# New figures for TensorE products and per-row scaling in a kernel that schedules itself

## The chip, the cores and the metric

One Trainium2 chip, one core of it, one launch. The metric is the time of the device in microseconds (us), median of several runs.

## The reference

```python
# attention: 2 batches x 8 heads x 768 positions x 64; 4 sink keys, window 128
scores = scale * np.matmul(q, k.transpose(0, 1, 3, 2))
scores = np.where(is_sink | in_window, scores, -1e9)
a = np.exp(scores - np.max(scores, axis=-1, keepdims=True))
a = a / (np.sum(a, axis=-1, keepdims=True) + 1e-09)
x = (a @ v).transpose(0, 2, 1, 3).reshape(1536, 512)
# mixture of 4 experts, w1 512x1024, w2 1024x512, all experts for all tokens
p = domain_probs / (domain_probs.sum(-1, keepdims=True) + 1e-09)
for e in range(4):
    out += p[:, e:e + 1] * (np.maximum(x @ w1[e], 0.0) @ w2[e])
# gated layer, d_ff 1536
return (out @ w_a) * (out @ w_b) @ w_out
```

The weights of the gated layer come as 64-bit floats, passed as pairs of 32-bit integers, and are turned into 32-bit floats on the chip.

## The kernel before

**The arithmetic.** Every operand of a product is split in two rounded parts, high and low (`split`, L467), and a product is three matmuls: high by high, high by low, low by high (`three`, L956). In the trace those are `xh,uh`, `xl,uh`, `xh,ul` or `dh,hh`, `dh,hl`, `dl,hh`. The products with w1, w_a and w_b go through `seven` (L1031), which makes a 2x2 block product from seven products, with 384 columns each. The products with w2 and w_out have 512 columns (`down_tile`, L973; `Gated.tile`, L1138). Attention is done with 256 to 288 columns (`scores`, L595); for batch 0 its score products take their 64 rows of contraction straight from one head (tiles `kk`, `qh`, `ql`), and the softmax rows are multiplied by the reciprocal of their sum, a number per row (tiles `pp`, `st`; L680 ff.). The 128x128 transposes are products with `ident`.

**The stages.** There are three, each recorded and then put in order by itself. Stage 1: attention of batch 0 and the first two chunks of the experts (TensorE instructions 1 to 672 of 4845, to about 119 us). Stage 2: attention of batch 1 beside 13 items of experts on batch 0 (to about 375 us). Stage 3: the last item of batch 0, 16 items of experts on batch 1, then 24 items of the gated layer. One item (`Expert` L1085, `Gated` L1105) is a block of 256 columns of w1, or of 128 of w_a and the same 128 of w_b, with the 768 tokens of a batch.

**The weights.** For each item `ups` (L912) loads a block of w1 (`rawu<-in_w`) or of the converted w_a and w_b (`rawu<-gu`), makes four sums on POOL or DVE (`sums`), and splits them on ACT, DVE and POOL (`uh`, `ul`). The buffer `rawu` is there once, so a load can start when the item before has read it. Split weights are stored for the second batch (`ug`, `dg` for the gated layer) and loaded back. `gate_weights` (L1251) converts the 64-bit weights in stage 3, part by part: load to `raw`, six operations on `tu` (mostly DVE, some on ACT and POOL), store to `gu` or `gd`. The first gated items read `gu` as it becomes ready.

**The order.** Nothing is issued where it is written. `Plan` (L95) records each call with its operands; `note` (L177) makes a node of it, finds what it depends on, and asks `cost` (L149) for its length in ns on each engine that may do it (`either`, L118: copies on ACT or DVE, sums on POOL or DVE, scaling on ACT, DVE or POOL). Codes are T for TensorE, V for DVE, S for ACT, G for POOL and D for a DMA. `run` (L244) then gives each node a due time, worked back from TensorE's nodes, whose own times are the sum of their costs; it steps through a model of the five engines, always placing the node that can start first, the most urgent among those ready, within 8 nodes of TensorE's written order. `fits` (L279) decides there between engines. The result is one fixed order for each engine's queue; every instruction of the kernel is issued from L355 in that order. Fixed figures of the model that stay as they are: the lag between engines (`LAG`, 60 to 256 ns, and `EXTRA` 40), 2200 ns from a DMA to its user (`WAY`), and the DMA issue itself, 60 ns + 1.42 per element of a row.

So the figures of `cost` say nothing to the chip. They decide in which order, on which engine, and how far ahead of TensorE the other work stands.

Of the kernel before, what the change touches and what calls it, by code (L numbers as in the profile page):

```python
# [18 lines left out]
P = 128  # L19
# [75 lines left out]
class Plan:  # L95
# [52 lines left out]
    @staticmethod  # L148
    def cost(engine, name, args, kw):  # L149

        size = 1
        for d in kw.get("out", args[0] if args else None).shape[1:]:
            size *= d
        psum = any("PSUM" in str(getattr(v, "space", "")) for v in (*args[1:], *(v for k, v in kw.items() if k != "out")))
        if engine == "T":
            return 3 + size / 2.4 * (2 if name == "transpose" else 1)
        if engine == "V":
            fast = name in ("tensor_copy", "tensor_scalar") and not psum
            return 65 + size * (0.52 if fast else 1.04) + (55 if fast and hasattr(kw.get("scalar1"), "ap") else 0)
        if engine == "S":  # L160
            return (50 if psum else 95) + size / 1.2 + (180 if "accum_out" in kw else 0)
        return {"G": 150 + size * 2.1, "D": 60 + size * 1.42}[engine]

    @staticmethod
# [79 lines left out]
    def run(self, ahead=8):  # L244
# [46 lines left out]
        for _ in nodes:  # L291
# [42 lines left out]
            for f in x["ways"]:  # L334
                ready[f].remove(x)
            x["e"], (cost, x["calls"], shared) = e, x["ways"][e]
            x["cost"] = cost
            free[e] = now + cost
# [1282 lines left out]
```

## Time and profile before

| | |
|---|---|
| median of 3 runs | 952.56 us (951.90 to 953.61) |
| the profiled execution, its own time | 951.72 us |
| its span | 949.6 us |
| TensorE (PE) busy | 920.8 us, 97% of the span, 4845 matmuls |
| DVE, ACT, POOL busy | 741.1 (78%), 404.3 (43%), 324.2 (34%) us |
| chain that ended last | PE 77%, DVE 13%, DMA 5%, ACT 2% |

The span is what the trace covers; the profiled execution took 2.1 us more than it, and 0.84 us less than the median. A record's length is not its share of an engine: matmuls overlap, so that a 512-column matmul has a record of 0.39 us while the next starts 0.23 us after it. What a product takes is therefore read from the distance of starts in the timeline.

### The profile page before, as it was taken

How to read it: one execution, taken by the hardware profiler on the slowest of the kernel's cores; microseconds unless marked ns; L12 is line 12 of the kernel's file. 1: busy time of each engine (PE TensorE's matmuls, PEld its weight loads, DVE VectorE, ACT ScalarE, POOL GpSimd, SP SyncE). 2: the span in 40 equal slices, each digit the busy share in tenths (PEclk: the TensorE clock that was granted, in tenths of full speed). 3: DMA queues.
4: the chain of work that ended last, by engine and by line, in shares of the span. 5: the costliest groups of instructions: out<-in, count | busy, mean ns of one | idle time of the engine just before them, and what ended most of it. 6: DMA issues, size and time to landing. Idle time of an engine off the chain costs nothing.

```text
span 949.6 us, 13937 instructions
## 1 busy us (share of the span) xinstructions
PE 920.8 (97%) x4845; PEld 824.8 (87%) x4845; DVE 741.1 (78%) x1516; ACT 404.3 (43%) x946; POOL 324.2 (34%) x328
## 2 busy tenths in 40 slices
PE   7999989999999999999999999999999999999996
PEld 6778878898888888888989989999887789999995
DVE  6798789999999998997876878799898985333343
ACT  6677557766656573521222312143453453211111
POOL 3565445646544651520200110044254543110100
PEclk9699999999999999999999999999999999999998
DMA  4250068886566744587867777877778878755552
GB/s 150 93 204 25 2 211 319 289 289 233 181 232 239 287 170 154 202 314 253 304 225 284 248 263 245 289 252 250 272 257 296 285 287 314 268 199 199 201 198 93
DMA packets 84752, 215.47 MB, mean 227 GB/s; under 512 B 7872, under 2 KB 42176, under 8 KB 84672
## 3 DMA queue, kind: packets, MB, share of 16 engines
q1 hardware_dynamic: 84672, 214.49, 64.6%
q8 instruction: 40, 0.66, 0.3%
q14 instruction: 40, 0.33, 0.1%
HBM read 131.10 MB, written 83.36 MB: 226 GB/s over the span
## 4 chain that ended last, share of the span: by engine, by line
PE 77%; DVE 13%; DMA 5%; ACT 2%; issue 2%; POOL 1%; SPq 1%; DVEq 0%; ACTq 0%; POOLq 0%
PE bank L355 77%; DVE tu L355 2%; DMA rawu<-gu 2%; DVE ul L355 2%; DVE y L355 1%; DVE kk L355 1%; DVE c L355 1%; DVE pp L355 1%; DVE sums L355 1%; DVE hl L355 1%; DMA rawu<-in_w 1%; DVE st L355 1%; DMA scr<-in_dp 1%; DMA araw<-in_a 1%; SPq L355 1%
## 5 line engine op out<-in xcount | busy, mean ns | idle before, releaser
L355 PE MATMUL bank<-dh,hh 128*128 128x512 f32 x528 | 210.2, 398 | 0.0
L355 PE MATMUL bank<-dl,hh 128*128 128x512 f32 x528 | 208.5, 395 | 0.0
L355 PE MATMUL bank<-dh,hl 128*128 128x512 f32 x528 | 208.0, 394 | 0.0
L355 PE MATMUL bank<-xh,uh 128*128 128x384 f32 (+1 forms) x384 | 129.7, 338 | 0.7 <-DVE r L355 0.7
L355 PE MATMUL bank<-xl,uh 128*128 128x384 f32 (+1 forms) x384 | 127.2, 331 | 0.0
L355 PE MATMUL bank<-xh,ul 128*128 128x384 f32 (+1 forms) x384 | 127.1, 331 | 0.0
L355 PEld LDWEIGHTS bank<-dl,hh 128*128 128x128 f32 x528 | 99.0, 187 | 21.7
L355 PE MATMUL bank<-th,uh 128*128 128x384 f32 x324 | 109.7, 339 | 3.9 <-DVE c L355 2.5
L355 PEld LDWEIGHTS bank<-dh,hh 128*128 128x128 f32 x528 | 99.2, 188 | 13.9 <-issue 0.3
L355 PEld LDWEIGHTS bank<-dh,hl 128*128 128x128 f32 x528 | 99.2, 188 | 12.6
L355 PE MATMUL bank<-tl,uh 128*128 128x384 f32 x324 | 109.2, 337 | 0.1
L355 PE MATMUL bank<-th,ul 128*128 128x384 f32 x324 | 108.8, 336 | 0.0
L355 ACT ACTIVATE r<-bank 128x384 f32<-128x384 f32 x73 | 35.8, 491 | 146.5 <-PE bank L355 145.9
L355 ACT ACTIVATE hh<-c 128x384 fp32r<-128x384 f32 x98 | 50.8, 519 | 96.7 <-DVE c L355 95.5
L355 DVE TENSOR_TENSOR c<-bank,r 128x384 f32<-128x384 f32 x108 | 59.8, 554 | 35.1 <-PE bank L355 34.5
L355 DVE SCALAR_TENSOR_TENSOR y<-bank,prob,y 128x512 f32<-128x512 f32 x108 | 80.0, 744 | 7.3 <-PE bank L355 6.6
L355 DVE TENSOR_TENSOR c<-bank,u 128x384 f32<-128x384 f32 x54 | 29.9, 553 | 67.6 <-PE bank L355 64.4
L355 PEld LDWEIGHTS bank<-xh,uh 128*128 128x128 f32 x384 | 72.7, 189 | 7.3 <-issue 1.1
L355 PEld LDWEIGHTS bank<-xl,uh 128*128 128x128 f32 x384 | 72.8, 190 | 4.4
L355 PEld LDWEIGHTS bank<-xh,ul 128*128 128x128 f32 x384 | 72.7, 189 | 0.0
L355 PEld LDWEIGHTS bank<-th,uh 128*128 128x128 f32 x324 | 60.8, 188 | 9.1 <-DVE c L355 3.7
L355 POOL TENSOR_TENSOR ul<-sums,uh 128x256 fp32r<-128x256 f32 (+1 forms) x39 | 40.6, 1043 | 80.7 <-ACT uh L355 80.6
(147 smaller groups left out, 1860.5 us busy)
## 6 DMA issues: line engine op xcount, KB each, us to landing
ue<-uh SPq DMA_DIRECT2D x14, 896.0 KB, 4.3
ue<-ul SPq DMA_DIRECT2D x14, 896.0 KB, 6.1
uh<-ue SPq DMA_DIRECT2D x14, 896.0 KB, 4.8
ul<-ue SPq DMA_DIRECT2D x14, 896.0 KB, 6.8
ug<-uh SPq DMA_DIRECT2D x12, 896.0 KB, 5.4
ug<-ul SPq DMA_DIRECT2D x12, 896.0 KB, 7.8
uh<-ug SPq DMA_DIRECT2D x12, 896.0 KB, 4.7
ul<-ug SPq DMA_DIRECT2D x12, 896.0 KB, 6.8
```

The lines of the kernel that those rows point to most:

```text
L355: call(*args, **kw)
```

## The change

Only `cost` is touched. A product of N columns goes from 3 + N/2.4 to 1 + 0.4535 N, a transpose of N columns from 3 + N/1.2 to 1 + 0.84 N, a product whose weights have fewer than 128 rows gets 65 ns more, and an ACT instruction with a scale per row gets 85 ns more. In ns: 512 columns 216.3, now 233.2; 384 columns 163.0, now 175.1; 256 columns 109.7, now 117.1; a transpose of 128 columns 109.7, now 108.5; 288 columns with 64 rows 123.0, now 196.6; per-row scaling of 288 columns on ACT 335, now 420.

```diff
@@ -153,12 +153,14 @@
         if engine == "T":
-            return 3 + size / 2.4 * (2 if name == "transpose" else 1)
+            rows = kw["lhsT"].shape[0] if "lhsT" in kw else P
+            return 1 + size * (0.84 if name == "transpose" else 0.4535) + (65 if rows < P else 0)
...
         if engine == "S":
-            return (50 if psum else 95) + size / 1.2 + (180 if "accum_out" in kw else 0)
+            return (50 if psum else 95) + size / 1.2 + (180 if "accum_out" in kw else 0) + (
+                85 if hasattr(kw.get("scale"), "ap") else 0)
```

No instruction is added or taken away in the arithmetic: the matmuls are the same 4845. What moves is order, and the engine of operations that may run on two: over the program DVE has 35 instructions more and ACT 40 fewer, of which 20 and 22 lie in stage 2.

**At the start, on DVE's queue.** `scr<-scr 128x12` is the sum of the four domain probabilities, which waits for their load; `pp<-bank,pen` (an ISA row) masks a tile of scores in PSUM and frees that bank for TensorE's next score products. Before:

```order
L355 TENSOR_TENSOR kk_157<-araw_146,kk_157 128x288
L355 TENSOR_SCALAR flag<-lim 128x1
L355 TENSOR_SCALAR scr_140<-lim 128x1 x2
L355 ISA pp_151,low<-bank_99,pen 128x288
L355 ISA low 128x1
L355 ISA pp_151,low<-bank_98,pen 128x128
L355 ISA low 128x1
L355 TENSOR_REDUCE scr_140<-scr_140 128x12
L355 TENSOR_SCALAR st_152<-st_152 128x2
```

and after:

```order
L357 TENSOR_TENSOR kk_157<-araw_146,kk_157 128x288
L357 TENSOR_TENSOR vv_147<-araw_145,vv_147 128x2x2x64
L357 TENSOR_REDUCE scr_140<-scr_140 128x12
L357 TENSOR_SCALAR flag<-lim 128x1
L357 TENSOR_SCALAR st_152<-st_152 128x2
L357 ISA pp_151,low<-bank_99,pen 128x288
L357 ISA low 128x1
L357 RECIPROCAL st_152<-st_152 128x2
L357 ISA pp_151,low<-bank_98,pen 128x128
```

The sum over the probabilities now stands ahead of both maskings, where it stood behind them; a subtraction for `vv` has come to DVE as well.

**Among the first gated items, on the queue of DMA issues (SP).** `rawu<-gu_66` is the load of the converted weights of one gated item; `raw<-in_wa` and `raw<-in_wo` are loads of 64-bit weights for the conversion and `gu_70<-tu` is a store of one half of a converted block; `ug`, `dg` are stores of split weights. Before:

```order
L355 DMA dg_1_3850<-dl_180 128x512
L355 DMA dg_0_3853<-dh_171 128x512
L355 DMA rawd_158<-gd_77 128x512
L355 DMA dg_1_3854<-dl_172 128x512
L355 DMA dg_0_3857<-dh_179 128x512
L355 DMA raw_1_3827<-in_wa 128x4x256
L355 DMA gu_70<-tu_3828 512x1x128
L355 DMA rawu_163<-gu_66 128x1024
```

and after:

```order
L357 DMA raw_0_3825<-in_wo 128x1024
L357 DMA rawd_158<-gd_76 128x512
L357 DMA dg_1_3849<-dl_180 128x512
L357 DMA dg_0_3852<-dh_171 128x512
L357 DMA rawu_163<-gu_66 128x1024
L357 DMA ug_0_3850<-uh_169 128x1792
L357 DMA raw_1_3826<-in_wa 128x4x256
L357 DMA ug_1_3851<-ul_170 128x1792
L357 DMA gu_70<-tu_3827 512x1x128
```

The load of the item's weights stood behind a load and the second store of the conversion and now stands ahead of them, and the stores of `dg` and the load `rawd<-gd_77` that stood ahead of it come later. Counted in TensorE instructions written before it, this load moves from 3694 to 3638; those of blocks 65 and 67 move from 3592 to 3580 and from 3767 to 3712, and that of block 64 goes back from 3516 to 3524.

## Rows read from the trace of the kernel before

**Rows 1.** The page: span, busy time by engine, chain by engine.

```profile
span 949.6 us, 13937 instructions
...
PE 920.8 (97%) x4845; PEld 824.8 (87%) x4845; DVE 741.1 (78%) x1516; ACT 404.3 (43%) x946; POOL 324.2 (34%) x328
...
PE 77%; DVE 13%; DMA 5%; ACT 2%; issue 2%; POOL 1%; SPq 1%; DVEq 0%; ACTq 0%; POOLq 0%
```

**Rows 2.** Busy time by stretch: length, then each engine, TensorE's granted clock, DMA share, GB/s.

```profile
core 0: us, PE busy (x) PEld busy (x) DVE busy (x) ACT busy (x) POOL busy (x), PEclk, DMA share, GB/s
0.00:23.74 23.74, 17.20 (x69) 14.65 (x69) 15.31 (x77) 14.35 (x45) 9.42 (x24) 1.00 0.50 150
118.69:142.44 23.75, 20.78 (x113) 18.53 (x112) 20.27 (x38) 12.89 (x31) 10.64 (x15) 1.00 0.61 212
142.44:356.10 213.66, 211.49 (x1145) 188.41 (x1144) 203.68 (x433) 142.51 (x352) 121.19 (x123) 1.00 0.71 249
660.00:780.00 120.00, 112.70 (x582) 100.99 (x581) 108.53 (x174) 55.56 (x118) 53.88 (x46) 1.00 0.79 275
28.96:46.02 17.06, 17.06 (x66) 14.56 (x66) 10.81 (x40) 10.22 (x31) 7.42 (x8) 0.50 0.31 96
```

**Rows 3.** Timeline of PE: start, length of the record, engine, line, operation.

```profile
23.31 0.52 PE L355 MATMUL bank<-kk,qh 64*128 64x288 f32 x2
23.68 0.29 PE L355 MATMUL bank<-kk,ql 64*128 64x288 f32 x1
...
60.66 0.40 PE L355 MATMUL bank<-dh,hh 128*128 128x512 f32 x1
...
61.82 0.39 PE L355 MATMUL bank<-dl,hh 128*128 128x512 f32 x1
...
502.49 0.33 PE L355 MATMUL bank<-th,uh 128*128 128x384 f32 x1
502.66 0.33 PE L355 MATMUL bank<-tl,uh 128*128 128x384 f32 x1
```

**Rows 4.** Groups: count | busy, mean ns | idle before, and what ended it.

```profile
L355 ACT ACTIVATE pp<-pp,st 128x288 f32<-128x288 f32 (+1 forms) x79 | 33.0, 470 | 15.9 <-DVE sq L355 6.0 <-DVE st L355 6.0 <-POOL sq L355 3.6
...
L355 PE MATMUL bank<-ident,pp 128*128 128x128 f32 x176 | 29.8, 294 | 2.2 <-ACT pp L355 1.7 <-DVE pt L355 0.5
```

**Rows 5.** Waits of PE from 660 to 780 us: total, times, longest.

```profile
PE bank L355 <- ACT r L355: 3.4, 3, 2.0
PE bank L355 <- DVE c L355: 1.4, 3, 0.9
PE bank L355 <- DVE ul L355: 1.4, 1, 1.4
PE bank L355 <- ACT x L355: 1.2, 2, 0.6
```

**Rows 6.** The chain that ended last, pieces from 677 to 771 us: start, length, what.

```profile
677.26 6.62 DMA rawu<-gu
...
688.81 0.48 ACT r L355
689.34 14.97 PE bank L355 x78
...
766.48 4.39 DMA rawu<-gu
```

**Rows 7.** Timelines of DVE and PE at the start, in brackets what ended the idle time.

```profile
8.68 0.45 DVE L355 CUSTOM_DVE_ANT_0 pp<-bank,pen 128x288 f32<-128x288 f32 x1
9.05 0.08 DVE L355 DVE_READ_ACCUMULATOR2_ANT low<- 128x1 f32 x1
...
10.70 0.20 DVE L355 TENSOR_REDUCE scr<-scr 128x12 f32<-128x48 f32 x1 [1.11 <-DMA scr<-in_dp]
...
9.28 0.81 PE L355 MATMUL bank<-kk,qh 64*128 64x288 f32 x2
...
11.85 0.88 PE L355 MATMUL bank<-ident,pp 128*128 128x128 f32 x3 [0.88 <-ACT pp L355]
```

## The prediction

> **What bounds the kernel now.** I read the page first: TensorE is busy 920.8 of 949.6 us, and the chain that ended last is TensorE for 77% [rows 1]. Nothing in the change makes a product shorter, and none is dropped, so all that can be won is time in which TensorE stands, 949.6 - 920.8 = 28.8 us, and what a changed order does to its clock. The second view is the busy time by stretch, which tells where it stands [rows 2]: 23.74 - 17.20 = 6.5 us at the start, 23.75 - 20.78 = 3.0 us where stage 1 hands over to stage 2, 213.66 - 211.49 = 2.2 us over the whole of stage 2 that follows, and 120.00 - 112.70 = 7.3 us between 660 and 780 us, where the gated items begin. These are 19.0 of the 28.8 us. The third view is the timeline of TensorE, for the true distance of products: six 512-column products start from 60.66 to 61.82, which is 1.16 / 5 = 0.232 us each; the 384-column ones start 0.17 us apart; two 64-row ones take 23.68 - 23.31 = 0.37 us, 0.185 each [rows 3]. The new figures (233, 175 and 197 ns) are these; the old ones (216, 163 and 123) were too short by 7% and by a third. The figure for scaling per row goes from 335 to 420 ns, towards a record of 470 in the mean [rows 4]. So the change makes the scheduler's TensorE run at the chip's pace. Before, the model's TensorE ran ahead of the real one; the other engines were planned against a faster engine than there is. A plan with too fast a TensorE shifts everything it cannot finish in time to the most urgent order and sees engines as full that are not. With a slower TensorE it sees more room per product on the other engines, and sets work earlier as counted in products.
>
> [...]
>
> **Part by part.** All five terms are changes of TensorE's standing time, since only order moves.
>
> *Start.* DVE used to mask the 288-column scores at 8.68, ahead of the sum over the probabilities, which waited 1.11 us for its load and ran at 10.70; the bank so freed let TensorE begin score products at 9.28 [rows 7]. Now the sum stands ahead, and DVE takes its queue in order: the masking can start at about 10.70 + 0.2 and two small operations, some 11.1, ends 0.45 later, and the products start at 11.5 instead of 9.28, 2.2 us later. Of this, 0.88 us is time in which TensorE would have waited anyway, before the transposes at 11.85 [rows 7]. That leaves 2.2 - 0.88 = **+1.3 us**. Bounds: 0, if the transposes' own chain stays in time and the products fit behind them; +2.2, if the softmax on ACT slips by as much as the masking.
>
> *Later softmax of stage 1.* The transposes stood for 2.2 us in all for `pp` and `pt`, 0.88 of it the wait just named [rows 4, 7], so 1.3 us are left, at two places. With 64-row products and scaling at their true length, the order puts more TensorE work between a scaling and its transpose there (7 instructions instead of 1 at the tightest). New places with 3 appear elsewhere. I take **-0.9**, with bounds -1.3 and 0.
>
> *Handover, 119 to 142 us.* TensorE stands 3.0 us [rows 2], waiting for DVE. Of DVE's operations there, one copy of a product's result goes to ACT, and one copy and one sum come to DVE. ACT is busy for 12.89 of 23.75 us there, DVE for 20.27. I take **-1.0**, a third; bounds -2.0 (one of the 3.0 us stays with loads that no figure moves) and 0.
>
> *Stage 2, 142 to 356 us.* DVE gets 20 instructions more, ACT 22 fewer. At DVE's mean of 203.68 / 433 = 0.47 us that is 9.4 us of work for an engine with 213.66 - 203.68 = 10.0 us left by its records [rows 2]. But records overlap: the masking of 8.68 lasts by its record to 9.13, and the next instruction starts at 9.05 [rows 7], 0.37 us after it, 18% less than 0.45. If all do so, DVE is held for 167 of 214 us, and 9.4 more fit. I take **0**; bounds -2.2 (all the standing time goes) and +9.4.
>
> *First gated items, 660 to 780 us.* TensorE's waits here sum to 3.4 + 1.4 + 1.4 + 1.2 = 7.4 us, for `r` and `x` from ACT, `c` and `ul` from DVE [rows 5]. They are late because ACT and DVE stand in their queues at splits of weights whose load has just landed: the chain goes through a load of 6.62 us at 677.26, ends with ACT's copy `r` at 688.81, and TensorE goes on at 689.34 [rows 6]. In the new order the loads of blocks 65, 66 and 67 stand 12, 56 and 55 TensorE instructions earlier. One instruction is 120.00 / 582 = 0.206 us here [rows 2], so these are 2.5, 11.5 and 11.3 us, more than any wait of this group. The load of block 64 goes back by 8, or 1.6 us; the longest wait, 2.0 us, hangs on it and stays. On the queue of DMA issues the load of block 66 now passes a store of the conversion, which comes later: that block of converted weights is ready later, and what is late next is a later gated item's load. I set 0.4 us for it, next to the smallest wait of the group (0.6). So 7.4 - 2.0 - 0.4 = 5.0, **-5.0 us**. Bounds: -7.3 (all of it) and 0 (the next rival).
>
> Elsewhere TensorE hardly stands, and I set nothing. Each engine's instructions there move within the time that TensorE covers; if that cover went, the price is that of stage 2's upper bound, which the first rival has.
>
> **Sum.** 1.3 - 0.9 - 1.0 + 0 - 5.0 = -5.6 us against the profiled execution's 951.72, which is 946.1. That execution is 0.84 us under the median of the runs, so I forecast 947.0 us as the median. The likely bounds of this case are 942 to 951.
>
> **The rivals.**
>
> *DVE becomes the bound in stage 2 (slower).* Place: 142 to 356 us. The 20 instructions more take 9.4 us, and 10.0 us are free by the records. From the point at which the free pieces are shorter than one instruction each, or lie where DVE waits for TensorE, the 9.4 us go through to TensorE, which waits there for `hl` and `c`. For it: DVE at 95%. Against it: the overlap, and that TensorE stood for only 2.2 us at that load. Time: 951.72 + 1.3 - 0.9 - 1.0 + 9.4 - 5.0 = 955.5, 956.4 as a median.
>
> *Nothing comes of stage 3 (no change).* The waits of 660 to 780 us hang on loads of 4.39 to 6.62 us [rows 6], and the scheduler still reckons with the same short time for them. If a load's issue is held by its buffer, an earlier place in the queue brings nothing. Then the handover and the gated items give 0, and the sum is +1.3 - 0.9 = +0.4: 952.1, 953.0 as a median. For it: the load is the longest piece of the chain there. Against: the waits sit behind the splits, which move apart from the loads.
>
> [...]
>
> *The figures overshoot.* If products took the 216 ns of the old formula wherever no record is missing, the new plan would set work 8% late against the real TensorE, and the standing time of 660 to 780 us would double: 951.72 + 1.3 + 7.3 = 960.3, 961.1 as a median. [...] Rows 3 are against it at three sizes.
>
> **How the numbers follow.** A measurement of this kernel can tell about 0.2%, 1.9 us, from no change: faster is below 950.7, slower above 954.5. Chances: the forecast 0.55; nothing from stage 3 0.17; DVE as the bound 0.17; the clock 0.09; overshoot 0.02. Faster: 0.50 of the forecast, 0.04 of the second, 0.09 of the clock, 0.63. Same: 0.05 and 0.10, 0.15. Slower: 0.17, 0.02 and 0.03 of the second, 0.22. The range of 940 to 956.5 leaves out two thirds of the clock's case, the lowest corner of the forecast, half of DVE's case and the overshoot, about 0.18.
>
> **What would show it.** Right: in the profile of the changed kernel TensorE is busy over 117 of the 120 us of the first gated items and the waits for `r`, `c` and `x` there are under 3 us; the score products of the second head start after 11 us. DVE in stage 2 is busy longer than before by some 9 us, and TensorE no less. Wrong: TensorE's busy time between 142 and 356 us falls by several us with waits for DVE (DVE as the bound); the waits in the gated items stay near 7 us (nothing from stage 3); the stretch of clock 0.50 is gone or longer (clock); products of 512 columns start nearer than 0.23 us (overshoot).

## The result, and the profile after

| | before | with the change |
|---|---|---|
| median | 952.23 us (8 runs, 949.05 to 957.55) | 960.53 us (8 runs, 959.96 to 963.64) |
| profiled execution, span | 951.72, 949.6 us | 961.12, 959.3 us |

The ratio is 1.0085, with a 95% interval of 1.0064 to 1.0105: the change makes the kernel 0.85% slower. The forecast was 947.0 with a range of 940 to 956.5, so the result lies outside the range and on the other side.

The head of the page with the change, for [rows 1]:

```profile
span 959.3 us, 13934 instructions
...
PE 925.5 (96%) x4845; PEld 822.6 (86%) x4845; DVE 756.3 (79%) x1551; ACT 387.4 (40%) x906; POOL 325.8 (34%) x332
...
PE 42%; DVE 33%; DMA 15%; issue 3%; POOL 3%; ACT 2%; SPq 1%; DVEq 0%; POOLq 0%; ACTq 0%
```

TensorE's part of the chain that ended last fell from 77% to 42%, DVE's rose from 13% to 33% and that of DMAs from 5% to 15%. Before, TensorE led and the rest kept up; now long pieces of that chain run through DVE and through transfers. Where time was lost, the busy time by stretch tells. With the change, for [rows 2]:

```profile
0.00:23.74 23.74, 15.00 (x56) 12.49 (x57) 13.89 (x68) 13.37 (x40) 10.28 (x24) 1.00 0.49 149
118.69:142.44 23.75, 21.92 (x118) 19.58 (x117) 20.41 (x40) 14.64 (x35) 10.42 (x14) 1.00 0.68 237
142.44:356.10 213.66, 208.59 (x1119) 183.65 (x1118) 207.06 (x435) 132.14 (x322) 116.04 (x119) 1.00 0.69 245
375.00:660.00 285.00, 281.25 (x1402) 249.27 (x1400) 237.83 (x426) 68.86 (x130) 43.78 (x35) 1.00 0.72 250
660.00:780.00 120.00, 118.22 (x607) 105.78 (x608) 110.04 (x174) 52.55 (x113) 62.68 (x55) 1.00 0.81 281
```

The fourth of these stretches was not looked at ahead of the change, since TensorE did not stand in it at all; in the trace of before it is

```profile
375.00:660.00 285.00, 285.00 (x1436) 256.53 (x1436) 235.53 (x416) 79.87 (x152) 55.37 (x45) 1.00 0.75 260
```

Read the counts in brackets rather than the busy time. In 142 to 356 us TensorE did 26 products fewer than before (1119 against 1145), in 375 to 660 us 34 fewer (1402 against 1436), and in 660 to 780 us 25 more (607 against 582). At 213.66 / 1145 = 0.187 us a product the first is 4.9 us, at 285.00 / 1436 = 0.198 the second is 6.7 us, both lost; at 0.206 us the third is 5.2 us won. The busy time shows only 2.9 and 3.75 us of the losses: a 512-column product has a record of 0.39 us and the next can start after 0.23, so a stop of up to 0.16 us hides in the record of the product ahead.

Since both programs have the same 4845 matmuls in nearly the same order, the loss can be followed exactly: take the start of TensorE's instruction n (counted from 0) in either trace and subtract. Against before, the change stands at -0.1 us at instruction 672 (end of stage 1), at +5.5 at 1994 (end of stage 2), at +12.7 at 3560 (685 us in before), at +7.0 at 3960, at +8.1 at 4100, and stays there to TensorE's last instruction. The span is 9.7 us longer: the other 1.6 us are lost behind that, while the last results are stored. That tail differs from before's by -0.3 to +1.9 us in the other runs, and none of them goes after it. The experiments below are told in these four pieces: **stage 1** (to 672), **stage 2** (672 to 1994), **early stage 3** (1994 to 3560) and **gated start** (3560 to 4100).

Three stops in early stage 3 show how products are lost there. One of them, in the timeline of all engines of the changed kernel:

```profile
422.67 0.39 PE L357 MATMUL bank<-dh,hh 128*128 128x512 f32 x1
...
422.89 0.39 PE L357 MATMUL bank<-dh,hl 128*128 128x512 f32 x1
...
423.13 0.40 PE L357 MATMUL bank<-dl,hh 128*128 128x512 f32 x1
...
423.34 0.74 DVE L357 SCALAR_TENSOR_TENSOR y<-bank,prob,y 128x512 f32<-128x512 f32 x1
...
424.00 0.68 DVE L357 TENSOR_TENSOR tu<-tu 128x512 f32<-128x512 f32 x1
...
424.23 0.34 PE L357 MATMUL bank<-xh,ul 128*128 128x384 f32 x1
...
424.60 0.55 DVE L357 TENSOR_TENSOR c<-bank,r 128x384 f32<-128x384 f32 x1
...
425.21 0.45 PE L357 MATMUL bank<-th,uh 128*128 128x384 f32 x1 [0.64 <-DVE c L357]
```

TensorE needs the bank that `c<-bank,r` reads. That stands on DVE behind a `y` and behind a step of the weight conversion (`tu<-tu`), each 0.6 to 0.7 us; DVE has no idle time there, it is only late. No transfer made it late: DVE's first wait for one in this stage ends at 438.01 us, and by then 3.1 of the 7.2 us are lost. One reason can be seen at an earlier stop, at 391.74 us. DVE in the trace of before, then all engines with the change:

```profile
382.14 0.95 DVE L355 TENSOR_TENSOR xl<-x,xh 128x768 fp32r<-128x768 f32 x1
383.09 0.56 DVE L355 TENSOR_TENSOR c<-bank,r 128x384 f32<-128x384 f32 x1
```

```profile
386.98 1.85 POOL L357 TENSOR_TENSOR tl<-x,th 128x768 fp32r<-128x768 f32 x1 [3.39 <-ACT th L357]
...
387.28 2.36 DVE L357 TENSOR_TENSOR xl<-x,xh 128x768 fp32r<-128x768 f32 x1
...
389.57 1.65 DVE L357 TENSOR_TENSOR x<-x 128x384 f32<-128x384 f32 x1
...
391.14 0.55 DVE L357 TENSOR_TENSOR c<-bank,r 128x384 f32<-128x384 f32 x1
...
391.74 0.44 PE L357 MATMUL bank<-th,uh 128*128 128x384 f32 x1 [0.75 <-DVE c L357]
```

With the change `xl` starts while POOL is at `tl`, and takes 2.36 us instead of 0.95; `c` stands behind it.

The other 4.1 us are lost after 438.01 us, and there DVE does stand for transfers. A stop of that kind:

```profile
570.75 0.43 DVE L357 TENSOR_SCALAR tu<-raw 128x512 int32<-128x512 int32 x1 [2.38 <-DMA gd<-tu]
...
572.88 0.55 DVE L357 TENSOR_TENSOR c<-bank,r 128x384 f32<-128x384 f32 x1
...
573.49 0.55 PE L357 MATMUL bank<-ident,y 128*128 128x128 f32 x3 [0.93 <-DVE c L357]
```

DVE's own waits for stores from 375 to 660 us, with the change and before:

```profile
DVE tu L357 <- DMA gu<-tu: 14.1, 10, 2.6
DVE tu L357 <- DMA gd<-tu: 7.0, 5, 2.4
```

```profile
DVE tu L355 <- DMA gu<-tu: 1.7, 4, 0.5
DVE tu L355 <- DMA gd<-tu: 1.4, 2, 0.9
```

The one buffer `tu` is free for the next part when its store has landed; DVE arrives at that part too early and stands, and all that is queued behind it stands with it.

At the start, for [rows 7], timelines of DVE and PE with the change:

```profile
10.82 0.20 DVE L357 TENSOR_REDUCE scr<-scr 128x12 f32<-128x48 f32 x1 [1.74 <-DMA scr<-in_dp]
10.94 0.14 DVE L357 TENSOR_SCALAR flag<-lim 128x1 f32<-128x1 f32 x1
11.00 0.79 DVE L357 TENSOR_SCALAR st<-st 128x2 f32<-128x2 f32 x1
11.70 0.45 DVE L357 CUSTOM_DVE_ANT_0 pp<-bank,pen 128x288 f32<-128x288 f32 x1
...
12.30 0.82 PE L357 MATMUL bank<-kk,qh 64*128 64x288 f32 x2 [2.90 <-DVE st L357]
```

The masking runs at 11.70 instead of 8.68, and TensorE takes up the second head at 12.30 instead of 9.28, as forecast but 0.8 us later still.

And the gain that was forecast is there. TensorE's waits from 660 to 780 us, for [rows 5]:

```profile
PE bank L357 <- ACT x L357: 0.6, 1, 0.6
PE bank L357 <- DVE r L357: 0.6, 1, 0.6
PE bank L357 <- ACT r L357: 0.5, 1, 0.5
PE bank L357 <- DVE c L357: 0.2, 1, 0.2
```

1.9 us where 7.4 stood.

### The profile page after: what moved, and what is told of

The parts are those of the page before. It is cut to its first block, busy times and chain, and to the rows that moved or that the text cites. A ratio compares the mean times of both kernels' runs of the same rounds, so it can differ in the third digit from the quotient of the medians.

```text
span 959.3 us, 13934 instructions
## 1 busy us (share of the span) xinstructions
PE 925.5 (96%) x4845; PEld 822.6 (86%) x4845; DVE 756.3 (79%) x1551; ACT 387.4 (40%) x906; POOL 325.8 (34%) x332
## 4 chain that ended last, share of the span: by engine, by line
PE 42%; DVE 33%; DMA 15%; issue 3%; POOL 3%; ACT 2%; SPq 1%; DVEq 0%; POOLq 0%; ACTq 0%
PE bank L357 42%; DVE tu L357 9%; DMA gu<-tu 6%; DVE y L357 4%; DVE hl L357 3%; DMA rawu<-in_w 3%; DVE c L357 3%; DMA rawu<-gu 3%; DVE ul L357 2%; DMA gd<-tu 2%; DVE sums L357 2%; POOL tu L357 1%; DVE x L357 1%; DVE kk L357 1%; POOL sums L357 1%
## 5 line engine op out<-in xcount | busy, mean ns | idle before, releaser
L357 ACT ACTIVATE hh<-c 128x384 fp32r<-128x384 f32 x94 | 48.8, 519 | 135.7 <-DVE c L357 135.6
L357 POOL TENSOR_TENSOR tu<-tu 128x512 f32<-128x512 f32 x15 | 19.7, 1311 | 177.4 <-DVE tu L357 177.4
```

The lines of the kernel that those rows point to most:

```text
L357: call(*args, **kw)
```

## The experiments

Three theories stood against each other at first. **Pace**: what counts in the table is TensorE's pace against that of the other engines; correcting TensorE alone takes the plan further from the chip. **Engines**: the copies and sums that moved to DVE are the loss. **Store wait**: in early stage 3 it is the wait for the store of `tu`. The expectations of e1 to e4 call the first one "margin": the other engines lose the lead that the short figure gave them, whether or not the ratio is then the true one. Each run was profiled, and its pieces are given here in us against the first profile of before; medians have their ratio to before, run on the same chip, and its 95% interval.

| run | stage 1 | stage 2 | early stage 3 | gated start | median | ratio |
|---|---|---|---|---|---|---|
| the change | -0.1 | +5.6 | +7.2 | -4.6 | 960.53 | 1.0085 (1.0064 to 1.0105) |
| e1 product alone | -6.1 | +3.2 | +7.1 | -3.3 | 953.64 | 1.0011 (0.9989 to 1.0034) |
| e2 64 rows, scaling alone | +2.3 | +1.3 | +0.7 | -1.6 | 954.37 | 1.0005 (0.9986 to 1.0023) |
| e3 all times 0.93 | +0.4 | -0.1 | 0.0 | +0.8 | 952.27 | 0.9979 (0.9961 to 0.9998) |
| e4 DMA 4500 ns | -8.6 | +0.9 | +5.1 | +8.0 | 960.99 | 1.0079 (1.0052 to 1.0107) |
| e5 shared operations slower | -8.0 | 0.0 | +10.3 | +10.7 | 966.15 | 1.0150 (1.0094 to 1.0206) |
| e6 DVE times 1.17 | 0.0 | +1.5 | +1.5 | +3.7 | 957.79 | 1.0060 (1.0030 to 1.0089) |
| e7 start in order | +3.6 | +5.3 | +9.2 | -3.4 | 959.54 | 1.0074 (1.0041 to 1.0108) |
| e8 two tu | 0.0 | +5.7 | +7.2 | -9.2 | 956.40 | 1.0052 (1.0026 to 1.0078) |
| e9 new figures, old engines | +2.6 | +5.2 | +6.2 | -1.7 | 964.06 | 1.0132 (1.0074 to 1.0189) |
| e10 old figures, new engines | +4.6 | +3.1 | +4.8 | +4.0 | 967.26 | 1.0156 (1.0106 to 1.0206) |
| e11 before, two tu | -1.0 | +3.6 | +1.5 | -9.7 | 943.87 | 0.9904 (0.9874 to 0.9934) |
| e12 times 0.93, two tu | -1.4 | -1.1 | +1.2 | -9.4 | 940.86 | 0.9887 (0.9838 to 0.9935) |
| e13 times 0.86, two tu | +1.3 | -0.2 | +2.5 | -7.2 | 948.01 | 0.9948 (0.9922 to 0.9973) |
| e14 less conversion | 0.0 | +5.4 | +6.1 | -7.6 | 955.11 (one run) | |
| e15 before again | -4.6 | +2.0 | 0.0 | -0.3 | 949.05 (one run) | |

The last line tells how to read the others. Stage 1 of one and the same program differs by 4.6 us between two executions, as TensorE's pace there does (its clock was granted at 0.50 for 17.06 us of stage 1 in the first profile [rows 2], and the mean of the whole execution is 0.988 there and 0.995 in e15); before ran from 947.5 to 958.8 us in 79 runs beside the experiments, with a mean granted clock of 0.983 to 0.997, the long ones at the low clock (958.79 us at 0.983, 947.47 at 0.996). Stage 2 differed by 2.0 us, and by 3.6 in e11, whose first two stages are those of before and whose granted clock was 0.94 from 120 to 147 us. Part of this goes with TensorE's clock. In e2, e6, e9, e11, e13 and e15 it was granted at 0.50 for 3.4 to 6.8 us near the start of stage 2 (in e15 from 132.24 to 135.65 us), and these runs are 1.1 to 2.7 us later by instruction 775; the first profile of before and that of the change have no such drop there. At the gated start it was granted at 0.50 for 3.4 us in e3, e6 and e9, for 6.8 in e4 and e10 and for 13.6 in e5, so that part of their loss there is likely the clock's. Early stage 3 and the gated start of before repeat within 0.3 us in e15. But e2, whose stage 3 has the order of before, instruction for instruction, has +0.7 and -1.6 there, and e7, whose plan there is the change's, has +9.2 and -3.4 where the change has +7.2 and -4.6. So these pieces can differ by 2 us.

**e1, the product figure alone.**

```diff
-            return 3 + size / 2.4 * (2 if name == "transpose" else 1)
+            return 3 + size / 1.2 if name == "transpose" else 1 + size * 0.4535
```

> Only the product figure is new (1 + 0.4535 N); transposes, 64-row products and scaling keep the old figures. Stage 3 comes out with the same number of instructions on each engine as with the whole change (DVE 739, ACT 317, POOL 113), stage 2 with half of the shift to DVE (501, against 491 before and 511 with the change). Theory 'margin' (the old product figure, 7% short, made the plan run every other engine ahead of TensorE; the true one takes that lead away): stage 2 loses most of the 6.9 us, 357 to 660 us the 7.2 us, 660 to 780 us gains 7.0; in all 957 to 961. Theory 'DVE in stage 2' (the 20 instructions moved are the loss): stage 2 loses half, about 3.5 us. Theory 'small figures' (64 rows and scaling do the harm): near 950 to 953.

The loss of early stage 3 is all there (+7.1) and so is the gain after it; stage 2 has 3.2 of 5.6 us. The median did not follow, since stage 1 took 6.1 us less in the profile: in this order DVE masks the second head in time, and TensorE's products were at their full pace from 29.4 us on, with the change only from 42 us (48 products in 29 to 36 us, 27 with the change). So the sum of stages 2 and 3, +6.9, is the product figure's, and the expected median was missed by what stage 1 gave. By the medians neither this half of the change nor the other one (e2) slows the kernel; only the pieces show the loss. Why stage 1 is shorter here is not shown: e7 has the start in order too and does not get it.

**e2, 64 rows and scaling alone.**

```diff
-            return 3 + size / 2.4 * (2 if name == "transpose" else 1)
+            rows = kw["lhsT"].shape[0] if "lhsT" in kw else P
+            return 3 + size / 2.4 * (2 if name == "transpose" else 1) + (65 if rows < P else 0)
...
-            return (50 if psum else 95) + size / 1.2 + (180 if "accum_out" in kw else 0)
+            return (50 if psum else 95) + size / 1.2 + (180 if "accum_out" in kw else 0) + (
+                85 if hasattr(kw.get("scale"), "ap") else 0)
```

> Only the 65 ns for 64 rows and the 85 ns for scaling are new; products and transposes keep the old figures. Stage 3 has the counts of before (724, 336, 109), stage 2 has 494 on DVE. Margin: 950 to 953 like before, stages 2 and 3 within 1 us of it; stage 1 may move by 1 to 3 us. Small figures: 957 to 961.

Nothing that they do to stages 2 and 3 can be told from the differences between executions: the +1.3 us of stage 2 are there at instruction 775, with the drop of the clock (138.06 to 141.47 us), and stage 3 is in the order of before. The late start, +2.2 us at the 25th product, comes with these figures.

**e3, all of TensorE's new figures times 0.93.**

```diff
-            return 1 + size * (0.84 if name == "transpose" else 0.4535) + (65 if rows < P else 0)
+            return (1 + size * (0.84 if name == "transpose" else 0.4535) + (65 if rows < P else 0)) * 0.93
```

> The whole change, but every TensorE figure times 0.93, so that the proportions among them are the new ones and the plan's TensorE is again 7% fast. Margin: the loss of 142 to 357 us (6.9) and of 357 to 660 us (7.2) goes, the gain of 660 to 780 us (7.0) goes too; 949 to 953. If the proportions matter and not the pace: 957 to 961.

Both losses and the gain are gone, to 0.8 us. The proportions of the new table do neither harm nor good in stages 2 and 3; its pace does.

**e4, the change with 4500 ns from a DMA to its user.**

```diff
-    WAY = 2200.0
+    WAY = 4500.0
```

> The change as it is, with the time from a DMA to its user set to 4500 ns where it was 2200. Theory 'store wait' (from 357 to 660 us DVE stands in its queue at the conversion's next part until the store of the one buffer tu has landed, 13 to 21 us in sum, and what TensorE needs stands behind it): the waits DVE tu <- DMA there fall from 21 to under 8 us and 5 to 7 us come back, 953 to 956. Margin: 142 to 357 us keeps its loss of 6.9, since loads are not what is late there; if the loss of 357 to 660 us stays as well, the store wait is not its cause, 958 to 961.

The waits of `tu` fell from 21.1 to 3.5 us (375 to 660 us). Early stage 3 still lost 5.1 us, 2.3 of them at a single product near 641 us that waits for `hl`; 2.6 are lost ahead of DVE's first wait for a transfer, at 500.40 us. Stage 2 lost only 0.9, which neither theory had. Then 8.0 us are lost at the gated start, 6.3 at one stop near 792 us for a split of weights (`uh`). With the waits nearly gone most of the loss stayed, so the store wait can be a part of it at most; the two halves of the expectation do not add up, and this run settles no more than that.

**e5 and e6, the other engines' figures.** The distances of back-to-back instructions on DVE from 125 to 375 us in the trace of before sum to 106.5 us where the table has 100.2, for those that read PSUM, and to 59.9 where it has 42.5 for those that read SBUF alone; together 1.17. Two groups with the change show the difference at one shape, by the mean of their records:

```profile
L357 DVE TENSOR_TENSOR pt<-bank,pt 128x512 fp32r<-128x512 f32 x32 | 21.9, 685 | 3.4 <-ACT pt L357 3.2
...
L357 DVE TENSOR_TENSOR ul<-rawu,uh 128x512 fp32r<-128x512 f32 x14 | 15.1, 1081 | 0.6 <-ACT uh L357 0.6
```

The table has one figure for both. By the sums above, operations from SBUF alone take 1.41 times the table and those that read PSUM 1.06 times. The length goes with POOL: by the records of these two groups, `ul` takes 679 ns in the mean of the 4 that no POOL instruction overlaps and 1241 in the mean of the 10 that one overlaps, while `pt`, which reads PSUM, takes 689 (8) and 683 (24). What makes it so is not shown, and no run here takes POOL's work away.

```diff
-            return 65 + size * (0.52 if fast else 1.04) + (55 if fast and hasattr(kw.get("scalar1"), "ap") else 0)
+            return (65 + size * (0.52 if fast else 1.04) + (55 if fast and hasattr(kw.get("scalar1"), "ap") else 0)) * (1.0 if psum else 1.4)
...
-        return {"G": 150 + size * 2.1, "D": 60 + size * 1.42}[engine]
+        return {"G": 175 + size * 2.46, "D": 60 + size * 1.42}[engine]
```

> The change, with the figures of DVE for operations that read no PSUM times 1.4 and those of POOL times 1.17, as back-to-back distances in the trace have them (DVE 59.9 us real against 42.5 by the table for such operations from 125 to 375 us). Stage 2 then has 482 instructions on DVE (491 before, 511 with the change). Theory 'pace' (what counts is TensorE's pace against that of the others; the others' figures are too short by more than TensorE's were, so correcting TensorE alone takes the plan further from the chip): the loss of stage 2 (5.6 us) and that from 357 to 685 us (7.2 us) go for the most part, as with all TensorE figures times 0.93: from TensorE instruction 672 on within 3 us of before, some 950 to 955. If a lead of the other engines was all that the old figure gave, and not a truer ratio, the result is the same; if instead the plan needs TensorE's figure itself short, 958 to 962.

e6 has `* 1.17` on the whole of DVE's line instead, and POOL's as it was.

> The change, with every DVE figure times 1.17 and POOL's as it is: the mean of real over table for DVE from 125 to 375 us. Stage 2 has 476 instructions on DVE. Pace: stage 2 within 2 us of before, 357 to 685 us within 4; 950 to 956. If it is the shared operations alone that the plan has wrong, it does worse than the run with these slowed, by 2 us or more.

Both bring stage 2 back (0.0 and +1.5). e6 brings early stage 3 back as well (+1.5 of 7.2). e5 does not: it loses 10.3 there and 10.7 at the gated start, so slowing just the operations that the trace has slow is no better table, against what I expected of it. (The model already keeps such operations of DVE and POOL apart, `shares` and `begin`, so that e5 may count the same wait twice; that was not tried.) That e6 should do worse than e5 was wrong. Neither is the time that "pace" forecast: e5 was to take 950 to 955 us and took 966.15, e6 950 to 956 and took 957.79, since it loses 3.7 us at the gated start where the change wins 4.6.

**e7, the start.**

```diff
                     if n == 12:
                         wide_ranges(scr)
...
-                        probabilities(scr)
                         sink_values(ab, 0)
+                    if n == 20:
+                        probabilities(scr)
```

> The change, with the sum over the probabilities written later in the recording (at step 20 of the first group where it was at 12), so that DVE masks the second head's scores before it waits for that load, as before the change; stages 2 and 3 have the counts of the change (511, 319, 134; 739, 317, 113). The 2.3 us that TensorE is late at its 25th instruction should go. Theory 'start' (the stop at 9 to 11.5 us also keeps TensorE's slow pace on, to 42 us where the profile before had 21 and a second slow stretch): stage 1 ends 4 to 8 us earlier, 953 to 957. If the slow pace does not hang on it: 2 us earlier or nothing, 958 to 961. Stages 2 and 3 lose the 8.2 us of the change in either case.

The 25th product is back to -0.01 us, but stage 1 ended 3.6 us later than in before: TensorE had its slow pace to 36.7 us and again from 44.2 to 54.5, there with a granted clock of 0.50. The profile is that of e7's longest execution (966.63 us; the ten go from 956.00 up). The late start is real and costs 2.4 us at its place; that the length of the slow stretch hangs on it is not shown.

**e8, the change with two buffers for `tu`.**

```diff
-bufs={"raw64": 2, "tu": 1}[name]
+bufs={"raw64": 2, "tu": 2}[name]
```

> The change, with two buffers for tu where it had one, so that the next part of the conversion needs not wait until the store of the last has landed. Stages 1 and 2 are those of the change. Theory 'store wait': the waits DVE tu <- DMA from 357 to 660 us (21 us with the change) fall to under 4, and of the 7.2 us lost from 357 to 685 us at least 4 come back; 955 to 957. If the loss stays, it is the lack of lead of c and y alone that TensorE waits for: 959 to 961.

Early stage 3 stays at +7.2. DVE no longer waits for the store; from 375 to 660 us it waits for the next part's load instead:

```profile
DVE tu L357 <- DMA raw<-in_wo: 7.5, 4, 2.1
DVE tu L357 <- DMA raw<-in_wb: 3.6, 3, 2.7
DVE tu L357 <- DMA raw<-in_wa: 1.8, 3, 1.2
DVE tu L357 <- DMA gd<-tu: 1.0, 1, 1.0
```

So the store as such is not the cause of the loss as a whole: 2.8 of the 7.2 us are lost here too before DVE waits for any transfer, at 437.74 us. The second buffer brought 4.6 us elsewhere, at the gated start, which was not expected and is used in e11 to e13. It is by this that the median came to 956.40, within what "store wait" forecast.

**e9 and e10, figures and engines crossed.** The engine of each operation that has a choice is written down from one plan, and the other plan's figures set the order.

```diff
+        for x, e in zip(free_choice, self.PINS[self.stage]):
+            x["ways"] = {e: x["ways"][e]}
```

> The order is planned with the change's figures, but every operation that may run on two engines is put on the engine that it had before (491 on DVE in stage 2, 724 in stage 3). The change lost 5.6 us in stage 2 and 7.2 us from 375 to 685 us, and won 4.6 us after. Theory 'engines' (the shift of copies and sums to DVE is the loss): both losses are gone to within 1.5 us each. Theory 'order' (the true pace sets other work ahead of what TensorE needs, whatever the engine): both losses stay to within 1.5 us. Median by engines 949 to 954, by order 958 to 962.

> The opposite: the order planned with the figures of before, every such operation on the engine that the change gave it (511 on DVE in stage 2, 739 in stage 3, 15 sums of tu on POOL). Theory 'engines': stage 2 loses 4 to 6 us and 375 to 685 us 5 to 7 us. Theory 'order': both within 1.5 us of before. Median by engines 956 to 962, by order 949 to 954.

With the new figures and the old engines both losses stay, 5.2 (1.1 of it by instruction 775, with the drop of the clock) and 6.2 us: the shift to DVE is not needed for them. The opposite run loses 3.1 and 4.8 us, so engines chosen by one plan fit another's order badly too; it does not clear them, it only shows that they are not the first cause. The gain at the gated start shrinks in e9 (-1.7), with 3.4 us at a granted clock of 0.50 in it: that the new engines help there is likely, not shown.

**e11 to e13, towards a better version.** e11 is before with two buffers for `tu`; e12 and e13 have the change's figures times 0.93 and times 0.86, and two buffers.

> The kernel before, with two buffers for tu. Stages 1 and 2 are those of before. With the change the second buffer gave 4.6 us more from TensorE instruction 3560 to 4100, where splits of weights and stores of the conversion meet; if that gain does not need the change's figures, 9 us of the 8.9 to 10 us that TensorE stands there before go, and 375 to 685 us stays at 0: 943 to 947, faster than both. If it needs them, 950 to 954; if the early loss comes with the larger count on DVE in stage 3 (759, the change 739), 950 to 956.

> All TensorE figures of the change times 0.93, and two buffers for tu. From TensorE instruction 672 on the run with 0.93 alone stood at +0.75 us against before; with the second buffer it should stand at -6 to -9: 943 to 947. If two buffers help only where the plan has TensorE's true pace, 951 to 954.

> Dose: all TensorE figures of the change times 0.86, two buffers for tu; with 0.93 the same kernel took 940.9 us. If a lead of the other engines over TensorE is all that counts, 0.86 gives as much or a little more: 938 to 942, stage 2 and 375 to 685 us as with 0.93. If 0.93 is near the true ratio of the table's paces and a plan can err on both sides, it loses again, as the change with DVE times 1.17 (the same ratio between DVE and TensorE) lost 3.7 us from TensorE instruction 3560 to 4100: 944 to 952.

e12 is the fastest, 940.86 us, 1.1% under before, though its interval overlaps with that of e11; TensorE's waits of [rows 5] have one line left in it:

```profile
PE bank L357 <- ACT x L357: 0.2, 1, 0.2
```

and its busy time in two of the stretches is

```profile
142.44:356.10 213.66, 212.45 (x1152) 189.62 (x1151) 204.23 (x436) 139.69 (x342) 125.14 (x128) 1.00 0.68 246
...
660.00:780.00 120.00, 119.69 (x630) 110.25 (x629) 96.62 (x181) 48.27 (x104) 38.90 (x37) 1.00 0.77 277
```

48 products more than before in the 120 us of the gated start. The last store of the conversion is issued at 706 us in e11, 701 in e12 and 690 in e8, where it is at 759 before and 765 with the change; in e13, at 754, it is late again in spite of the second buffer. e13 has 2.2 us less of the gain and loses 1.3 more in early stage 3. Each is about what one plan's pieces differ by, so that one can err on the other side as well is likely, not shown.

**e14, load or blocked queue.**

```diff
-            nc.vector.scalar_tensor_tensor(
-                out=u, in0=h, scalar=-0x40000000, in1=u, op0=ALU.bitwise_and, op1=ALU.bitwise_or
-            )
...
-            nc.vector.scalar_tensor_tensor(
-                out=uf, in0=tf, scalar=W_LOW * W_LOW, in1=uf, op0=ALU.is_ge, op1=ALU.mult
-            )
```

> The change with two of the five or six operations left out that each part of the conversion of the 64-bit weights does on DVE (the joining of the exponent bits and the zeroing of tiny numbers); the store and the wait for it stay. DVE has some 43 us less to do from 375 to 780 us. Stage 3 alone is of interest. Theory 'load' (DVE falls behind its plan since its operations last longer than the table has them): of the 7.2 us lost from TensorE instruction 1994 to 3560, 5 or more come back. Theory 'blocked queue' (DVE stands at the next part until the DMA it needs has landed, whatever its load): 5 or more stay, and the waits DVE tu <- DMA stay at 15 us or more.

DVE is busy for 215 us from 375 to 660 us instead of 238, and stands the longer:

```profile
DVE tu L357 <- DMA gu<-tu: 20.6, 15, 3.6
DVE tu L357 <- DMA gd<-tu: 12.7, 8, 3.7
```

6.1 of the 7.2 us stay, as "blocked queue" has it, but they are not the same 6.1. Up to DVE's first wait for a store, at 424.36 us here, 1.6 us are lost where the change lost 3.1: about half of that piece goes with DVE's load. Behind it DVE stands for stores for longer than with the change, 33.3 us against 21.1, and TensorE has a stop of 1.7 us at 460.33, behind a wait of 3.6. Both theories have a part.

**e15, before again**, for the differences between executions.

> The kernel before, unchanged, for a second profile of it. It tells how far the times of stages 2 and 3 of one and the same program differ between executions: the before with two tu has the same first two stages and yet took 3.6 us more in stage 2, with a granted clock of 0.94 from 120 to 147 us. Expected: stage 2, 375 to 685 us and the part behind within 1.5 us of the first profile where the clock is full; stage 1 may differ by 5 us and more.

**What holds, put together.** For each DVE instruction, take the TensorE instructions that had started when it ended, less those that stand before it in the planned order. That is how far DVE is behind its plan. The median of it for TensorE instructions 1994 to 3000: before 4, e2 4, e3 4, e6 4, e11 4, e12 4, e13 3, e15 4; the change 8, e1 8, e7 8, e8 8, e9 7, e14 8. The first eight lose 0 to 2.5 us in early stage 3, the last six 6.1 to 9.2. Three runs do not fit: e4 (4), e5 (5) and e10 (4) lose 5.1, 10.3 and 4.8 us there. So it goes with the loss where the pace of TensorE's figures is what differs, and is not the whole of it. Nor are the waits for stores: e6 has 13.9 us of them from 375 to 660 us and loses 1.5. The reading that fits best: with TensorE's true pace the plan sets DVE's work as if DVE kept to its figures and a DMA took 2200 ns; DVE is slower than its figure beside POOL (`ul` 1241 ns against 679, above), or stands at the conversion's transfers, and is twice as far behind. What share of the 7.2 us each of the two has is open. That TensorE's pace in the plan is the cause, e1 and e3 show, which bring the loss and take it away.

## Why the prediction was wrong

The premise failed, not a size. The prediction said that the old product figure was too short and the new one is the chip's; that holds, 512-column products start 0.23 us apart after as before (422.67 to 423.13 us above; [rows 3]), and the "overshoot" rival, whose time of 961.1 was the nearest, has no part in it: that it came near is luck. From this it went on to "with a slower TensorE it sees more room per product on the other engines, and sets work earlier", and took the earlier place as a gain alone. e3 and e6 show what was left out: it is the ratio of TensorE's figures to DVE's that counts. With either TensorE's 7% shorter or DVE's 17% longer, stage 2 and early stage 3 lose 1.5 us each at most. The trace has DVE's figures short by 1.17 in stage 2, so the old error of 7% on TensorE made up for part of it, and the true pace on one engine made a plan that the others can't keep. That it has to be the true ratio, and not just some lead of the others, is not shown: e5 is nearer to the trace than e6 and loses 10.3 us in early stage 3.

Step by step:

- *Start, +1.3, bounds 0 and +2.2.* Measured +2.4 at the 25th product. The mechanism was right; "two small operations, some 11.1" was short, since `st` alone took 0.79 us and the masking came at 11.70.
- *Later softmax, -0.9.* From the 25th product to instruction 672 the profiles differ by -2.5 us, but a second profile of before differs from the first by more than that in stage 1. It can't be told.
- *Handover, -1.0.* -1.3 from instruction 672 to 775, and the same in e7, e8 and e14 with the same plan. Right in size, against an execution of before without the drop of the clock.
- *Stage 2, 0, bounds -2.2 and +9.4.* +5.6 from instruction 672 to 1994, handover included (5.3, 5.7 and 5.4 in the three other runs with the same plan), 3.6 against the second profile of before, whose clock dropped in the handover. DVE was busy 3.4 us longer from 142 to 356 us, not 9, and TensorE 2.9 us less, with waits for `pt`, `y` and `low` from DVE instead of `hl` and `c`. The bound was wide enough and its rival named the place, but gave the shift of 20 instructions as the reason; e9 has the loss without the shift. The step "records overlap, and 9.4 more fit" counted DVE's time over the whole stretch, where the question is which instruction DVE does late.
- *Gated items, -5.0.* +25 products in 660 to 780 us, 5.2 us, and waits of 1.9 us where "under 3" was set. Right in size and place, and the reason fits: in the runs whose plan has the load of block 66 at TensorE instruction 3654 or earlier (the change, e1, e7 to e9, e11 to e14) the piece is won, by 1.7 to 9.7 us; in e3 to e6 and e10, which have it at 3674 or later, 0.8 to 10.7 are lost. (e2 has it where before has it, and its -1.6 is within what one plan's pieces differ by.)
- *"Elsewhere TensorE hardly stands, and I set nothing."* This is the step that cost most: +7.2 us in early stage 3. TensorE stood for nothing there before, DVE was busy for 235.53 of 285 us and the conversion was in its queue, with 3.1 us of waits for its stores. The prediction named what would follow "if that cover went" and put the price of another stretch on it, with no chance of its own. The order of the change was looked at where TensorE had stood, and not here, where DVE's queue came to be twice as far behind its plan.
- *The clock*, with a chance of 0.09 and a part in the range. Its sign, that the stretch of 0.50 is gone, came in, but no time with it: products were at the slow distance (0.21 us for 256 columns) from the start to 42 us, and stage 1 ended where it had. What such a stretch costs no run shows by itself.
- *Sum.* Measured by pieces: -0.1 + 5.6 + 7.2 - 4.6 = +8.1 on the profiles, and 1.6 behind TensorE's last product, for which the sum has no term and no run shows the cause. The forecast's own terms give -5.6, with the first gated items alone of the right size and sign beside the handover.

## To carry to other kernels

A planner's figures work by their ratio, and a truer table is not yet a faster plan. Here TensorE's figures set to the trace lost 0.85%; with a longer time for transfers, or with DVE's figures brought nearer to the trace as well, the kernel stayed 0.6 to 1.5% slower than before. With the ratio kept (TensorE times 0.93) it took about the time of before (0.2% less). So after such a change look at how far each engine runs behind its plan. Stretches where the bound engine never stands are the ones with something to lose; follow there what a new order puts on the queues that feed it, and count instructions per stretch, since busy time hides stops shorter than a record's overlap (0.16 us for 512 columns here). And read a piece's difference beside that of the same order run twice. What did help was a second buffer for the block under conversion: 0.96% in the old plan (e11), with the conversion done 53 us sooner.

## What was not expected of the hardware

In both traces the granted clock says nothing of the start. With the change, from 13 to 42 us, products start at 1.8 times the distance they have later (256 columns: 0.213 us apart from 40.44 to 41.29 us, 0.118 from 47.11 to 48.05), while the view gives a granted clock of 1.00 for that stretch:

```profile
28.69 1.65 PE L357 MATMUL bank<-pt,vv 128*128 128x256 f32 x6
30.13 0.84 PE L357 MATMUL bank<-ident,pp 128*128 128x128 f32 x3
```

Six products of 256 columns take 1.44 us, 0.24 each. Before, six of them at 22.41 us took 0.90, and the twelve at 38.20 us, at a granted clock of 0.50 [rows 2], 2.69 or 0.22 each:

```profile
22.41 0.97 PE L355 MATMUL bank<-pt,vv 128*128 128x256 f32 x6
23.31 0.40 PE L355 MATMUL bank<-kk,qh 64*128 64x288 f32 x1
...
38.20 2.76 PE L355 MATMUL bank<-pt,vv 128*128 128x256 f32 x12
40.89 0.85 PE L355 MATMUL bank<-kk,qh 64*128 64x288 f32 x2
```

So the distance with the change is about that at a granted clock of 0.50. The 1.00 is no reading: the first record of the clock in the trace stands at 42.28 us with the change and at 22.13 us before, just where products come to their full pace (256 columns 0.12 us apart from 42.73 and from 22.63 us on), and the view counts what lies ahead of it as full. What was granted there is not recorded; that it was 0.50 is likely, not shown. Where the slow stretches lie changed with nearly every run (to 42 us with the change, to 36.7 and from 44.2 to 54.5 in e7, to 22 and from 28.96 to 46.02 in before), and before went from 947.5 to 958.8 us between executions of one program; why the change's executions all lie within 3.7 us of each other and before's do not is open. Also open is whether the conversion, with a third buffer for its loads beside the second `tu`, would lose nothing in early stage 3 at TensorE's true pace: it was not tried.
